# Router logits of two steps summed in PSUM and selected by two products: a retention and two-level expert kernel

## The chip, the cores and the metric

The kernel runs on one core of one Trainium2 chip. The metric is the device time of the whole program in microseconds (us), as the median of several runs. A profiled execution is traced by the hardware profiler; its span, and the time of every instruction in it, count from its first to its last record. TensorE is PE in the rows (PEld for its weight loads, which run beside its products), VectorE is DVE, ScalarE is ACT, GpSimd is POOL, and SyncE, whose queue issues nearly all DMA, is SP.

## The reference

A retention attention (4 batches, 8 heads, 768 tokens, heads of 64 wide) makes x, 3072 tokens of 512 columns. Each token then chooses one of 4 groups and in it one of 4 experts, and is sent through that one expert alone.

```python
for t in range(S):                                    # per batch and head
    state = gamma * state + k[t] v[t]^T
    y[t] = scale * q[t] state
x = y, tokens of all batches x (H*D)                  # 3072 x 512
g_logits = x @ w_group                                # 4 logits
e_logits = x @ w_expert[g]                            # 4 logits for each of 4 groups
g, e = argmax of g_logits, argmax of e_logits of group g
out = softmax(g_logits)[g] * softmax(e_logits)[e] * (relu(x @ w1[g, e]) @ w2[g, e])
```

So each token has 20 router logits: 4 of the groups and 16 of the experts. They are what the change is about.

## The kernel before, in words

**The steps.** The attention runs in 12 steps i = 0 to 11. A step has 256 tokens, as two blocks u = 0 and 1 of 128 tokens; six steps (NC) make up one pass over the 768 tokens for half of the batches. In a step TensorE does, in the order in which the loop of `attention` writes it:

- `scores(i + 1, 0)` and `scores(i + 1, 1)`: the score products of the next step (L240) into the four PSUM banks `sh[0]` to `sh[3]`, two for each block. VectorE then masks each bank into `pf` (L252). In the rows the four banks are sh, in the order sh_116 to sh_119.
- `state_out(i, u)` (L291) and `value_out(i, u)` (L304): the output of the step, summed in PSUM as op, on four 64 x 64 quadrants and on halves of TensorE.
- `state_mm` (L266): keys times values into the state stp, which ScalarE copies to V (L276). The keys kk are transposed on TensorE and copied by ScalarE (`keys_mm`, L225, L226), but for steps 9 and 10 (KEYED), whose keys are loaded a second time, by DMA (L217), into the one buffer that kk has.
- `logits_mm(i - 1)` (L324): the router logits of the step before, see below, and their copy `ls` by ScalarE (L329).
- `out_x(i)`: VectorE scales op to `xt` (L316), the step's x, 512 columns in four groups of 128 rows by its 256 tokens. xt has two buffers.
- `trans_mm(i - 1)`: xt is transposed into the banks sh[2] and sh[3] (L350), ScalarE copies it to `xr` (L358), and a DMA writes it to memory as `xd` (L361), from which the tokens of an expert are gathered later. For step 10 that copy goes to a buffer of pf.

**The logits before.** The router weights `wr` are 128 x 4 x 32 (20 of the 32 columns in use). For each of the four groups j of x's columns one product of 32 stationary columns and 256 moving ones (the tokens) goes to its own 32 rows of PSUM:

```python
nc.tensor.matmul(
    lt[32 * j:32 * j + 32, :], self.wr[:, j, :], s["xt"][:, j].rearrange("p u t -> p (u t)"),
    start=True, stop=True, skip_group_check=True,
)
```

So the four partial sums of a logit stand in four row groups. `select_mm` (L337) adds them up and turns the result to tokens by logits: for each block the 128 x 128 piece of ls is the stationary operand and a constant of 128 x 20, which is 1 where row s has s % 32 equal to the column (`C_SEL`), the moving one. It writes 20 columns of the bank `log`. In most steps it stands inside `trans_mm`; in four steps it is held back as `late` and done in the next step by `select_late`. The product of the last step goes to a bank lgt of its own, with the tag "sta".

**Routing.** A batch is four blocks, two steps. `route` is a list of stages that `route_steps` lets run on from places in the loop: the maxima and marks on VectorE (from the logits in `log`, with the exponential ex on ScalarE, L396, and the marks oh, L408), the ranks on TensorE (L444, L446), the offsets on VectorE (L452 to L461), the weights. `spread` makes the lists' marks (hot on VectorE, ent on GpSimd, yT on VectorE) and `tally` (L555) counts them up on TensorE into the lists from which the tokens are gathered.

**Expert weights beside it.** Through all of this the expert weights come in as wf by DMA and are split in two parts: wh by ScalarE (L784), wl by VectorE (L786). The first expert layer (L918) starts after step 11; the first gather (L821) and its transposes (L839) stand ahead of it.

**What sets the order.** The schedule is manual: each engine does its instructions in the order in which the program writes them. SP's queue, too, issues the loads and the writes of xd in that order. A tile with one buffer is written again only when its last reader is done; the program waits on semaphores for that.

Of the kernel before, what the change touches and what calls it, by code (L numbers as in the profile page):

```python
# [51 lines left out]
C_DESC = C_TB + NL  # L52
C_SEL, C_SEG = C_DESC + 20, C_DESC + 40
C_KP, C_WP, C_IT = C_SEG + NX, C_SEG + 2 * NX, C_SEG + 3 * NX
# [17 lines left out]
def constants():  # L72
    s = np.arange(P)
    g = 1.0 - 2.0 ** (-5.0 - np.arange(H))
    c = np.zeros((P, C_REST + C_END), np.float64)
    n = np.arange(NC)[None, :, None] * P + KEYS.T[:, None, :] + 1.0
    c[:, C_GV:C_GV + NC * H] = (g ** -n).reshape(P, NC * H)
    for half in range(2):
        c[64 * half:64 * half + 64, C_GS:C_GS + 4] = g[[h[half] for h in HEAD]] ** P
    d = c[:, C_REST:]  # L80
    d[:, C_IO:C_IO + P] = s[None, :]
    d[:, C_PI] = s
    d[:, C_CH:C_CH + NCH] = P * (np.arange(NCH) - 32)
    d[:, C_TB:C_TB + NL] = (np.arange(NX)[:, None] * CAP + np.arange(2) * P).reshape(-1)
    d[:, C_DESC:C_DESC + 20] = [4, 3, 2, 1] * 5
    d[:, C_SEL:C_SEL + 20] = s[:, None] % 32 == np.arange(20)[None, :]
    d[:, C_SEG:C_SEG + NX] = np.arange(NX) * CAP
    d[:, C_KP:C_KP + NX] = np.arange(NX)
    d[:, C_WP:C_WP + NX] = PW
    d[:, C_IT:C_IT + MAXI] = np.arange(MAXI)  # L90
    return c.astype(np.float32)
# [20 lines left out]
class Kernel:  # L112
    def __init__(self, tc, qkv, kt, wr, w1p, w2p, cst, dec, out):
# [6 lines left out]
        self.held = None  # L120
        self.late = None
        self.waiting = False
# [186 lines left out]
    def out_x(self, i):  # L309

        s = self.st[i]
        s["xt"] = xt = self.wp.tile([P, 4, 2, P], F32, name="xt", bufs=2)
        for par in range(2):
# [3 lines left out]

    def logits_mm(self, i, bank=None):

        nc, s = self.nc, self.st[i]  # L320
        lt = self.pp.tile([P, 512], F32, name="lgt", tag="sta", bufs=1) if bank is None else self.sh[bank]
        lt = lt[:, 0:2 * P]
        for j in range(4):
            nc.tensor.matmul(  # L324
                lt[32 * j:32 * j + 32, :], self.wr[:, j, :], s["xt"][:, j].rearrange("p u t -> p (u t)"),
                start=True, stop=True, skip_group_check=True,
            )
        s["ls"] = self.wp.tile([P, 2 * P], F32, name="ls", bufs=1)
        nc.scalar.activation(s["ls"], lt, AF.Copy)  # L329

    def select_mm(self, i):

        nc, s = self.nc, self.st[i]
        for u in range(2):
            a = LG + 20 * (i % 2 * 2 + u)
            lg = self.log[:, a:a + 20]
            nc.tensor.matmul(lg, s["ls"][:, u * P:u * P + P], self.rest[:, C_SEL:C_SEL + 20], start=True, stop=True)  # L337

    def select_late(self):
        if self.late is not None:  # L340
            self.select_mm(self.late)
            del self.st[self.late]
            self.late = None

    def trans_mm(self, i, pool=None, late=False):

        nc, s = self.nc, self.st[i]
        for u in range(2):
            for j in range(4):
                nc.tensor.transpose(self.sh[2 + u][:, j * P:j * P + P], s["xt"][:, j, u], self.ident)  # L350
        if not late:
            self.select_mm(i)
        if i == NS2 - 2:
# [814 lines left out]
    def attention(self, extra, beside):  # L1168
# [27 lines left out]
        for i in range(NS2):  # L1196
# [10 lines left out]
            if i:  # L1207
                if i > 2:
                    self.outs(i)
                if i > 1:  # L1210
                    scores(i + 1, 0)
                if i % 2 and not last:
                    self.select_late()
                if i in (5, 7, 9):
                    self.tally()
                if i > 2:
                    self.state_out(i, 0)
                if last:
                    self.select_late()
                if i > 1:  # L1220
                    self.state_out(i, 1)
                if i < NS2 - 2:
                    self.select_late()
                if i % 2 == 0:
                    self.route_steps(99, True)
                if i > 1:
                    scores(i + 1, 1)
            self.load("q", i + 3)
            self.load("v", i + 3)
# [9 lines left out]
            self.state_copy(i)  # L1239
            if i == 10:  # L1240
                self.select_late()
            beside(i, 4)
            if i:
                self.logits_mm(i - 1, 1 if last or i % NC == NC - 2 or i + 1 in KEYED else 2)
            self.out_x(i)
# [26 lines left out]
            if i:  # L1272
                late = i + 1 in KEYED or i % NC == NC - 2
                self.trans_mm(i - 1, late=late)
                if late:
                    self.late = i - 1
                else:
                    del self.st[i - 1]
            if last:
# [27 lines left out]
    def run(self):  # L1307
        tc, nc = self.tc, self.nc
        with ExitStack() as ctx:
# [87 lines left out]
            hot = self.marks(p)  # L1397
            self.logits_mm(last)
            self.xtrans(ua, "big", (0,))
            self.select_mm(last)  # L1400
            self.trans_mm(last, self.yp, late=True)
            self.wload(va, 2)
# [161 lines left out]
```

## Time and profile before

| | us |
|---|---|
| median of 3 runs | 394.56 (394.51 to 395.0) |
| the profiled execution | 392.61 |
| its span | 390.9 |
| TensorE, products | 381.9 busy, 98% of the span |
| TensorE, weight loads | 322.9, 83% |
| VectorE | 288.5, 74% |
| ScalarE | 224.3, 57% |
| GpSimd | 160.2, 41% |

The mean granted clock of TensorE is 0.994 of full speed. The attention with the routing of the first five batches takes the span up to about 103 us; the rest are expert layers.

How to read the views. The view by windows gives a stretch, its width, the busy time of PE, PEld, DVE, ACT and POOL with the instructions of each, the granted clock of TensorE (1.00 is full), the share of time in which the 16 DMA engines were busy, and GB/s. The DMA view gives output and input, queue, the number of issues, the size of each and the median time from issue to landing. The chain of waits goes back from the last instruction to what released it, at each step; the timeline lists groups of alike instructions by their start, with their length. A bracket behind a row is the idle time of the engine ahead of it and what ended it.

### The profile page before, as it was taken

To read this page: it belongs to the slowest core of one execution; us is meant where nothing else is said; L and a number is where in the kernel's file an instruction comes from. 1 tells how busy PE (TensorE), PEld (TensorE's weight loads), DVE (VectorE), ACT (ScalarE), POOL (GpSimd) and SP (SyncE) were. 2 spreads that over 40 slices of the span, in tenths; PEclk is the share of its full clock that TensorE was granted. 3 is DMA by queue.
4 is the path that set the end of the run, shared out by engine and by line. 5 is a ranking of instruction groups with operands and counts; after the bars stand their busy time and mean duration, and the time that the engine had idled before them with its cause. 6 is when DMAs were issued, how large, how long until landed. Compare 5 with 4: busy or idle time off the path is not lost.

```text
span 390.9 us, 14282 instructions
## 1 busy us (share of the span) xinstructions
PE 381.9 (98%) x5945; PEld 322.9 (83%) x5977; DVE 288.5 (74%) x480; ACT 224.3 (57%) x342; POOL 160.2 (41%) x172
## 2 busy tenths in 40 slices
PE   8999999999999999999999999999999999999993
PEld 4888989888869888888888879797887978879792
DVE  3675876868879979795868686776878769788630
ACT  2234534544654766666657667676766767667620
POOL 5533669578766325131425324241531403322112
PEclk9999999999999999999999999999999999999997
DMA  7999999989647998787879797988879798797011
GB/s 254 342 369 325 315 381 321 341 292 305 221 177 259 338 359 269 249 278 257 268 249 274 268 331 251 300 294 305 293 262 352 273 314 300 268 349 263 6 49 50
DMA packets 38042, 107.24 MB, mean 274 GB/s; under 512 B 11415, under 2 KB 11543, under 8 KB 30548
## 3 DMA queue, kind: packets, MB, share of 16 engines
q1 hardware_dynamic: 28752, 92.52, 68.5%
q0 software_dynamic: 8928, 12.63, 9.2%
q8 instruction: 54, 0.88, 0.9%
q10 hardware_dynamic: 292, 1.08, 0.8%
q14 instruction: 16, 0.13, 0.1%
HBM read 94.18 MB, written 13.20 MB: 275 GB/s over the span
## 4 chain that ended last, share of the span: by engine, by line
PE 83%; issue 9%; POOL 3%; DMA 3%; DVE 0%; POOLq 0%; ACT 0%; SPq 0%; DVEq 0%; ACTq 0%
PE hps L918 19%; PE yps L1011 16%; PE hps L898 9%; PE yps L1016 6%; PE op L304 5%; PE sh L240 4%; PE yps L1004 3%; PE tpx L839 3%; PE sh L350 3%; PE stp L266 3%; PE op L291 2%; POOL out L1098 2%; DMA kk<-kt 2%; PE sh L324 1%; PE yps L955 1%
## 5 line engine op out<-in xcount | busy, mean ns | idle before, releaser
L786 DVE TENSOR_TENSOR wl<-wf,wh 128x1024 bf16<-128x1024 f32 x120 | 145.3, 1222 | 38.5 <-ACT wh L784 38.2
L784 ACT ACTIVATE wh<-wf 128x1024 f16<-128x1024 f32 (+1 forms) x136 | 133.6, 1002 | 1.0 <-DMA wf<-w2p 1.0
L918 PE MATMUL hps<-xbh,wh 128*128 128x0 bf16 x544 | 93.3, 241 | 0.0
L918 PE MATMUL hps<-xbh,wl 128*128 128x0 bf16 x544 | 93.3, 241 | 0.0
L1098 POOL DMA_INDIRECT out<-yo,mt x18 | 22.2, 1235 | 102.9 <-ACT yo L1078 100.1
L918 PEld LDWEIGHTS <-wh 128*128 128x128 f16 x616 | 56.5, 98 | 0.1
L925 ACT ACTIVATE hh<-hps 128x256 bf16<-128x256 f32 (+16 forms) x68 | 34.2, 503 | 35.6 <-PE hps L918 35.3
L918 PEld LDWEIGHTS <-wl 128*128 128x128 bf16 x544 | 53.2, 98 | 0.2
L898 PE MATMUL hps<-xbl,wh 128*128 128x256 f16 (+14 forms) x472 | 50.2, 249 | 0.0
L1016 PEld LDWEIGHTS <-wh 128*128 128x128 f16 x448 | 28.6, 97 | 24.9
L252 DVE TENSOR_TENSOR pf<-sh,tri 128x512 f32<-128x512 f32 x48 | 30.6, 685 | 21.8 <-PE sh L240 7.8
L1011 PE MATMUL yps<-wh,hl 128*128 128x512 f16 x112 | 42.5, 380 | 0.0
L1011 PE MATMUL yps<-wl,hh 128*128 128x512 bf16 x112 | 42.4, 379 | 0.0
L1011 PE MATMUL yps<-wh,hh 128*128 128x512 f16 x112 | 42.4, 378 | 0.0
L821 POOL DMA_INDIRECT xg<-xd,mt x22 | 36.8, 1674 | 11.0 <-PE hps L898 2.7
L841 ACT ACTIVATE xbh<-tpx 128x512 bf16<-128x512 f32 (+14 forms) x32 | 16.7, 523 | 42.7 <-PE tpx L839 42.6
L898 PEld LDWEIGHTS <-wh 128*128 128x128 f16 x472 | 40.2, 98 | 0.5
L1016 PEld LDWEIGHTS <-wl 128*128 128x128 bf16 x448 | 28.6, 97 | 13.3
L928 DVE SCALAR_TENSOR_TENSOR hl<-hps,hh 128x216 f16<-128x216 f32 (+15 forms) x64 | 36.8, 576 | 2.7 <-ACT hh L925 2.6
L1098 POOL DMA_INDIRECT out<-yo,gx x8 | 9.5, 1194 | 55.6 <-ACT yo L1078 41.4
L1016 PE MATMUL yps<-hh,wh 128*128 128x0 bf16 x448 | 31.8, 192 | 0.0
L1016 PE MATMUL yps<-hh,wl 128*128 128x0 bf16 x448 | 31.7, 192 | 0.0
(210 smaller groups left out, 632.6 us busy)
## 6 DMA issues: line engine op xcount, KB each, us to landing
wf<-w2p SPq DMA_DIRECT2D x29, 1024.0 KB, 6.3
wf<-w1p SPq DMA_DIRECT2D x28, 1024.0 KB, 6.9
lq<-qkv SPq DMA_DIRECT2D x24, 256.0 KB, 5.8
lk<-qkv SPq DMA_DIRECT2D x24, 256.0 KB, 5.3
lv<-qkv SPq DMA_DIRECT2D x24, 256.0 KB, 5.8
xd<-xr SPq DMA_DIRECT2D x22, 256.0 KB, 4.9
wf<-w1p SPq DMA_DIRECT2D x16, 256.0 KB, 5.9
wf<-w2p SPq DMA_DIRECT2D x8, 256.0 KB, 5.9
```

The source lines that it names most:

```text
L252: nc.vector.tensor_tensor(o, sc, tri, ALU.mult)
L304: nc.tensor.matmul(s["o"][par][64 * half:64 * half + 64, u, pp], s["vs"][:, u, hs], s["pf", u][:, par, p, :], start=(c == 0 and u == 0 and ...
L784: nc.scalar.activation(u["wh"][i][:, cs], u["wf"][i][:, cs], AF.Copy)
L786: (eng or nc.vector).tensor_tensor(u["wl"][i][:, cs], u["wf"][i][:, cs], u["wh"][i][:, cs], ALU.subtract)
L821: nc.gpsimd.indirect_dma_start(out=xg[0:r, i, :], out_offset=None, in_=self.xd[0:n, :], in_offset=bass.IndirectOffsetOnAxis(ap=mt[0:r, i, ...
L898: nc.tensor.matmul(hv[:, a, 0:w], l, xl[:, k, 0:w], start=(k == 0 and a == 0), stop=False, skip_group_check=True)
L918: nc.tensor.matmul(o, l[:, k, fs], m, start=(n == 0 and not arms), stop=(n == len(terms) - 1), skip_group_check=True,)
L925: nc.scalar.activation(hh[:, f, 0:W], hv[:, :, 0:W], AF.Relu)
L928: nc.vector.scalar_tensor_tensor(*rest)
L1011: nc.tensor.matmul(big, h[:, k, 0:P], w[k], start=(n == 0), stop=(n == 23))
L1016: nc.tensor.matmul(o, w[k][:, d * P:d * P + P], m, start=(n == 0 and d == 0), stop=(n == 23), skip_group_check=True,)
L1098: s = nc.gpsimd.indirect_dma_start(out=self.out, out_offset=bass.IndirectOffsetOnAxis(ap=mt[0:r, i, 0:1].bitcast(U32), axis=0), in_=yo[0:r ...
```

## The change

Three things are changed.

- **The products.** `pair_logits(i - 2)` takes the place of `logits_mm`. It runs in even steps i only, behind `scores(i + 1, 1)` and ahead of `value_out`, and does the logits of two steps, i - 2 and i - 1. Each of the four blocks of 128 tokens (two steps, two blocks) has its own 32 rows of PSUM, and the four column groups of x are summed there, in four products of 128 moving columns: 16 products in all. The result is 128 x 128, in bank sh[0]; that of the last pair, after the loop, is in lgt. ScalarE's copy ls is 128 x 128.
- **The selection.** `pair_select` takes the place of `select_mm` and `select_late`. It runs behind `state_copy` of even steps. With 64 columns of ls, twice, as the stationary operand and 80 columns of the unit matrix as the moving one, it turns the logits of 64 tokens of four blocks at once. `trans_mm` has no selection any more.
- **The constants.** `C_SEL` goes, 20 columns of 128 x 4 bytes, 10 KB.

```diff
-    def logits_mm(self, i, bank=None):
-        nc, s = self.nc, self.st[i]
-        lt = self.pp.tile([P, 512], F32, name="lgt", tag="sta", bufs=1) if bank is None else self.sh[bank]
-        lt = lt[:, 0:2 * P]
-        for j in range(4):
-            nc.tensor.matmul(
-                lt[32 * j:32 * j + 32, :], self.wr[:, j, :], s["xt"][:, j].rearrange("p u t -> p (u t)"),
-                start=True, stop=True, skip_group_check=True,
-            )
-        s["ls"] = self.wp.tile([P, 2 * P], F32, name="ls", bufs=1)
-        nc.scalar.activation(s["ls"], lt, AF.Copy)
-    def select_mm(self, i):
-        nc, s = self.nc, self.st[i]
-        for u in range(2):
-            a = LG + 20 * (i % 2 * 2 + u)
-            lg = self.log[:, a:a + 20]
-            nc.tensor.matmul(lg, s["ls"][:, u * P:u * P + P], self.rest[:, C_SEL:C_SEL + 20], start=True, stop=True)
+    def pair_logits(self, i):
+        nc = self.nc
+        if i == NS2 - 2:
+            lt = self.pp.tile([P, 512], F32, name="lgt", tag="sta", bufs=1)[:, 0:P]
+        else:
+            lt = self.sh[0][:, 0:P]
+        for g in range(4):
+            for j in range(4):
+                nc.tensor.matmul(
+                    lt[32 * j:32 * j + 32, :], self.wr[:, g, :], self.xts[i + j // 2][:, g, j % 2],
+                    start=(g == 0), stop=(g == 3), skip_group_check=True,
+                )
+        self.ls = self.wp.tile([P, P], F32, name="ls", bufs=1)
+        nc.scalar.activation(self.ls, lt, AF.Copy)
+    def pair_select(self):
+        pick = self.ident.rearrange("p (j c) -> p j c", j=4)[:, :, 0:20]
+        for a in (0, 64):
+            lg = self.log[a:a + 64, LG:LG + 80].rearrange("p (j c) -> p j c", j=4)
+            self.nc.tensor.matmul(lg, self.ls[:, a:a + 64], pick, start=True, stop=True, skip_group_check=True)
...
-        if not late:
-            self.select_mm(i)
...
                 if i > 1:
                     scores(i + 1, 1)
+                if i % 2 == 0:
+                    self.pair_logits(i - 2)
...
             self.state_copy(i)
-            if i == 10:
-                self.select_late()
+            if i and i % 2 == 0:
+                self.pair_select()
             beside(i, 4)
-            if i:
-                self.logits_mm(i - 1, 1 if last or i % NC == NC - 2 or i + 1 in KEYED else 2)
             self.out_x(i)
...
-            self.logits_mm(last)
+            self.pair_logits(last - 1)
             self.xtrans(ua, "big", (0,))
-            self.select_mm(last)
-            self.trans_mm(last, self.yp, late=True)
+            self.pair_select()
+            self.trans_mm(last, self.yp)
```

TensorE's order at two places. First step 10, from the last score product of step 11 (lq and lk are its queries and keys, sh_119 is bank sh[3]) to the tally. Before:

```order
L240 MATMUL sh_119<-lq,lk 64x64
L304 MATMUL op<-pf,vs 64x128 x16
L266 MATMUL stp<-vs,kk 64x64 x16
L337 MATMUL log<-rest,ls 128x20 x2
L324 MATMUL sh_117<-xt,wr 32x256 x4
L555 LDWEIGHTS hot
```

And of the changed kernel, where sh_116 is bank sh[0]:

```order
L239 MATMUL sh_119<-lq,lk 64x64
L326 MATMUL sh_116<-xt,wr 32x128 x16
L303 MATMUL op<-pf,vs 64x128 x16
L265 MATMUL stp<-vs,kk 64x64 x16
L338 MATMUL log<-ident,ls 64x80 x2
L548 LDWEIGHTS hot
```

The logits product has moved from behind the state product to ahead of value_out, as one of 16 instructions, into the bank in which the first scores of step 11 stand until VectorE's mask has read them.

Then the end of step 11 and what stands ahead of the first expert layer (lgt is the last product's bank, tpx the transposes of the gathered tokens xg, wh the expert weights). Before:

```order
L350 MATMUL sh_118<-ident,xt 128x128 x4
L350 MATMUL sh_119<-ident,xt 128x128 x4
L337 MATMUL log<-rest,ls 128x20 x2
L324 MATMUL lgt<-xt,wr 32x256 x4
L839 MATMUL tpx<-ident,xg_80 128x128 x4
L337 MATMUL log<-rest,ls 128x20 x2
L350 MATMUL sh_118<-ident,xt 128x128 x4
L350 MATMUL sh_119<-ident,xt 128x128 x4
L918 LDWEIGHTS wh
```

And of the changed kernel:

```order
L345 MATMUL sh_118<-ident,xt 128x128 x4
L345 MATMUL sh_119<-ident,xt 128x128 x4
L326 MATMUL lgt<-xt,wr 32x128 x16
L832 MATMUL tpx<-ident,xg_80 128x128 x4
L338 MATMUL log<-ident,ls 64x80 x2
L345 MATMUL sh_118<-ident,xt 128x128 x4
L345 MATMUL sh_119<-ident,xt 128x128 x4
L911 LDWEIGHTS wh
```

The selection behind the transposes of step 10 is gone, and the last product, now of steps 10 and 11, has 16 instructions in place of 4. On VectorE the mask that reads bank sh[0] in step 10 stands, before as now, behind the offsets of the ranks (L452 to L461), the weights of the batch and the marks for the lists (yT and hot). On VectorE, ScalarE, GpSimd and SP the order is as before, but that the copies ls are six in place of twelve and move with their products.

## Rows read from the trace of the kernel before

**Rows 1.** The page, section 1: busy time, share of the span, instructions

```profile
PE 381.9 (98%) x5945; PEld 322.9 (83%) x5977; DVE 288.5 (74%) x480; ACT 224.3 (57%) x342; POOL 160.2 (41%) x172
```

**Rows 2.** The view by windows, 6 to 84 us (columns: section on profile)

```profile
6.00:84.00 78.00, 77.36 (x1770) 68.24 (x1764) 52.99 (x125) 31.84 (x64) 47.78 (x62) 1.00 1.00 343
```

**Rows 3.** The DMA view, 6 to 84 us: count, size, median us to landing

```profile
lv<-qkv SPq DMA_DIRECT2D x22, 256.0 KB, 5.8
...
kk<-kt SPq DMA_DIRECT2D x2, 256.0 KB, 6.3
```

**Rows 4.** The DMA view, 100 to 104 us

```profile
xd<-pf SPq DMA_DIRECT2D x2, 256.0 KB, 2.1
```

**Rows 5.** The chain of waits, steps 7 to 10: start us, us, what

```profile
71.27 0.36 PE log L337 x4
...
76.03 0.93 PE stp L266 x32
...
77.59 6.23 DMA kk<-kt
...
83.87 1.33 PE stp L266 x32
...
92.25 0.55 PE log L337 x4
```

**Rows 6.** The waits of the weight loads, 0 to 105 us: us, times, longest

```profile
PEld stp L266 <- DMA kk<-kt: 0.3, 1, 0.3
```

**Rows 7.** The timeline, steps 2 to 4: start us, us, engine, line, instruction

```profile
29.31 0.16 PEld L324 LDWEIGHTS sh<-xt,wr 128*32 128x32 f32 x8
...
29.32 0.64 PE L324 MATMUL sh<-xt,wr 128*32 128x256 f32 x8
...
29.88 0.85 PEld L225 LDWEIGHTS sh<-ident,lk 128*128 128x128 f32 x8 [0.41 <-issue]
...
40.92 0.90 PEld L291 LDWEIGHTS op<-lq,V 64*64 64x64 f32 x32
```

**Rows 8.** The timeline, end of step 9 to the first expert layer

```profile
83.06 1.29 DVE L252 TENSOR_TENSOR pf<-sh,tri 128x512 f32<-128x512 f32 x2 [2.10 <-PE op L304]
...
86.63 0.20 PE L444 MATMUL log<-oh,stri 128*128 128x80 bf16 x1
...
87.52 0.22 DVE L452 TENSOR_TENSOR log<-log,nb 128x64 f32<-128x64 f32 x1
...
89.35 1.73 PEld L304 LDWEIGHTS op<-pf,vs 128*64 128x64 f32 x32
...
91.05 2.47 DVE L252 TENSOR_TENSOR pf<-sh,tri 128x512 f32<-128x512 f32 x4
...
94.28 1.08 ACT L358 ACTIVATE xr<-sh 128x512 f32<-128x512 f32 x2 [0.45 <-PE sh L350]
...
95.25 1.15 ACT L784 ACTIVATE wh<-wf 128x512 f16<-128x512 f32 x2
...
96.63 0.24 ACT L396 ACTIVATE ex<-log 128x80 f32<-128x80 f32 x1 [0.23 <-PE op L291]
...
97.94 0.23 DVE L408 TENSOR_TENSOR oh<-log,go 128x64 bf16<-128x64 f32 x1
...
98.97 0.10 PEld L444 LDWEIGHTS <-stri 128*128 128x128 bf16 x1 [0.41 <-issue]
...
99.31 0.23 DVE L452 TENSOR_TENSOR log<-log,nb 128x64 f32<-128x64 f32 x1
...
101.75 0.52 PEld L337 LDWEIGHTS log<-rest,ls 128*128 128x128 f32 x4 [0.21 <-ACT ls L329]
...
103.02 0.10 PEld L918 LDWEIGHTS <-wh 128*128 128x128 f16 x1
```

**Rows 9.** The view by windows, near the end of the span

```profile
387.00:388.00 1.00, 0.00 (x0) 0.00 (x0) 0.00 (x0) 0.00 (x0) 0.00 (x0) 0.50 0.28 111
```

**Rows 10.** The instructions of line 324 (xt product): shortest, median, longest ns

```profile
L324 PEld LDWEIGHTS sh<-xt,wr x88: 106/108/110, 19.4 to 98.4; 128*32 128x32 f32 x88
```

More of the change, by code (lines that the diff above doesn't have):

```diff
@@ L52 @@
 C_DESC = C_TB + NL
-C_SEL, C_SEG = C_DESC + 20, C_DESC + 40
+C_SEG = C_DESC + 20
 C_KP, C_WP, C_IT = C_SEG + NX, C_SEG + 2 * NX, C_SEG + 3 * NX
@@ L85, in constants @@
     d[:, C_DESC:C_DESC + 20] = [4, 3, 2, 1] * 5
-    d[:, C_SEL:C_SEL + 20] = s[:, None] % 32 == np.arange(20)[None, :]
     d[:, C_SEG:C_SEG + NX] = np.arange(NX) * CAP
@@ L120, in __init__ @@
         self.held = None
-        self.late = None
+        self.xts = {}
         self.waiting = False
@@ L311, in out_x @@
         s = self.st[i]
-        s["xt"] = xt = self.wp.tile([P, 4, 2, P], F32, name="xt", bufs=2)
+        s["xt"] = self.xts[i] = xt = self.wp.tile([P, 4, 2, P], F32, name="xt", bufs=2)
         for par in range(2):
@@ L316, in out_x, with trans_mm @@
             self.nc.vector.tensor_tensor(xt[:, gs], s["o"][par].rearrange("p u g t -> p g u t"), g, ALU.mult)
-    def logits_mm(self, i, bank=None):
-        nc, s = self.nc, self.st[i]
-        lt = self.pp.tile([P, 512], F32, name="lgt", tag="sta", bufs=1) if bank is None else self.sh[bank]
-        lt = lt[:, 0:2 * P]
-        for j in range(4):
-            nc.tensor.matmul(
-                lt[32 * j:32 * j + 32, :], self.wr[:, j, :], s["xt"][:, j].rearrange("p u t -> p (u t)"),
-                start=True, stop=True, skip_group_check=True,
-            )
-        s["ls"] = self.wp.tile([P, 2 * P], F32, name="ls", bufs=1)
-        nc.scalar.activation(s["ls"], lt, AF.Copy)
-    def select_mm(self, i):
-        nc, s = self.nc, self.st[i]
-        for u in range(2):
-            a = LG + 20 * (i % 2 * 2 + u)
-            lg = self.log[:, a:a + 20]
-            nc.tensor.matmul(lg, s["ls"][:, u * P:u * P + P], self.rest[:, C_SEL:C_SEL + 20], start=True, stop=True)
[L339 to L345, printed above, removed]
+    def pair_logits(self, i):
[17 more added lines that the diff above has]
+            self.nc.tensor.matmul(lg, self.ls[:, a:a + 64], pick, start=True, stop=True, skip_group_check=True)
+    def trans_mm(self, i, pool=None):
         nc, s = self.nc, self.st[i]
@@ L1211, in attention @@
                     scores(i + 1, 0)
-                if i % 2 and not last:
-                    self.select_late()
                 if i in (5, 7, 9):
@@ L1217, in attention @@
                     self.state_out(i, 0)
-                if last:
-                    self.select_late()
                 if i > 1:
                     self.state_out(i, 1)
-                if i < NS2 - 2:
-                    self.select_late()
                 if i % 2 == 0:
@@ L1239, in attention @@
             self.state_copy(i)
-            if i == 10:
-                self.select_late()
+            if i and i % 2 == 0:
+                self.pair_select()
             beside(i, 4)
-            if i:
-                self.logits_mm(i - 1, 1 if last or i % NC == NC - 2 or i + 1 in KEYED else 2)
             self.out_x(i)
@@ L1272, in attention @@
             if i:
[L1273 to L1278, printed above, removed]
+                self.trans_mm(i - 1)
+                del self.st[i - 1]
             if last:
```

## The prediction

> **What bounds the kernel now.** I read the page first. The reader is to see that TensorE counts as busy for 98% of the span [rows 1], which would make every TensorE instruction taken away a gain. So I next asked what paces the stretch that the change touches, steps 0 to 11 (to about 103 us). The view by windows answers: from 6 to 84 us the 16 DMA engines are busy for a share of 1.00 at 343 GB/s [rows 2]. They are not only busy but backed up: in that stretch a 256 KB load lands 5.8 us after its issue (median of 22), the keys of step 9 (kk) 6.3 us after it [rows 3], while a 256 KB write issued when the engines are idle lands after 2.1 us [rows 4]. The chain of waits shows where the backlog meets TensorE: one step of it is no TensorE work but the load of kk for step 9, 77.59 to 83.82, behind which state_mm(9) starts at 83.87 [rows 5]. TensorE waited only 0.3 us for it [rows 6], so two paths arrive together: TensorE's own and the DMA's. All loads and writes stand in SP's queue in one order that the change leaves alone, and so do their bytes (the constants shrink by 10 KB, under 0.03 us). Engines that are busy all the time don't finish the same bytes sooner because they are asked sooner. I take kk of step 9 to land at 83.8 as before.
>
> **What the change takes from TensorE.** A logits product of one step holds TensorE from 29.31 to the next load at 29.88 [rows 7]: 0.57 us, 12 times, 6.8 us. A selection costs 0.36 us on the chain where it stands behind the transposes, 0.55 us where it stands late [rows 5]; four of the twelve are late ones, so about 5 us. New are six logits products of a pair: 16 matmuls of 128 columns on four column groups. The nearest row is state_out, 16 matmuls of 128 columns on four 64 x 64 quadrants, whose loads span 0.90 us [rows 7]. The other end is the old product scaled by its columns: twice 0.57, 1.14 us. I take 1.0, the nearer to state_out since its columns agree. The new selection is two products of 64 stationary and 80 moving columns: at most the old 0.36 us; at least 0.12 us, four of the 32 passes that state_mm does in 0.93 us (76.03 in [rows 5]; two passes make one fp32 product). I take 0.27, nearer to the old one, since two products in a row hide little. Six pairs: 7.6 us against 11.8 us before, so TensorE loses 4.2 us of work. ScalarE's copy of the logits becomes one of 128 columns for two of 256; it is on no path that I found.
>
> The four column groups do overlap in the trace: all eight weight loads of an old product are issued within 0.16 us of 29.31, and eight passes take 0.64 us in all [rows 7]. [...]
>
> **Up to 83.87: nothing.** By state_mm(9) TensorE is rid of eight logits products (4.6 us) and six or seven selections (some 2.7 us) and has four pairs more (5.1 us): 2.2 us ahead, less what it loses to short waits for VectorE on the way, some 2 us. All of it ends in the wait for kk of step 9. Gain 0, at most the 0.3 us by which it waited already.
>
> **From 83.87 on, step by step against the old trace** [rows 8].
> - Step 9 ends without its logits product: the ranks (L444) stand at 86.05 in place of 86.63. VectorE is ready for them: its mask for step 10 waited for value_out(9), which is now about 2 us earlier, so the marks (oh) and xt(9) are done before the ranks.
> - A new wait. In step 10 the pair product of steps 8 and 9 is written into bank sh[0], and the scores of step 11 are still in that bank until VectorE's mask has read them. Its order there is unchanged: after the ranks come offsets, weights, the list marks and then the mask. Before, from L452 at 87.52 to the end of the first of four masks was 91.05 + 0.62 - 87.52 = 4.15 us. L452 can now start about 0.35 us after the ranks (98.97 to 99.31 shows that step), at 86.4, so the bank is free at 90.55. TensorE is there 2.72 us after the ranks (86.63 to 89.35), at 88.77, and waits 1.8 us. Queued behind it: value_out(10), state_mm(10), the selection, the tally, the transposes of xt(9). A gain is excluded, since the order on VectorE stands; I keep 1.3 us (half a microsecond less for marks that GpSimd slows) to 2.9 us (VectorE not ahead, the bank free at 91.67 as before).
> - So value_out(10) starts at 90.55 + 1.0 = 91.55, 2.2 us later than 89.35.
> - From there to ScalarE's copies xr(9) it was 4.93 us (to 94.28); a late selection and a logits product go (1.12 us), the new selection comes (0.27): 4.1 us, xr(9) at 95.6, 1.35 late.
> - ScalarE does in order xr(9), the weights wh, then the exponential ex. Before, ex did not wait for wh (95.25 + 1.15 = 96.40) but for VectorE, at 96.63. Now wh ends at 97.75 and ex starts at 97.8: 1.2 us late. The marks (oh) end 1.54 us behind the start of ex, at 99.35, in place of 98.17.
> - The last ranks waited for nothing at 98.97, since a logits product stood ahead of them; now they wait for oh until 99.4: 0.45 late.
> - From these ranks to the first expert layer (L918) it was 4.05 us. Out go a selection (0.55), a logits product (0.57), a selection (0.36) and a wait of 0.2 for ScalarE; in come a pair (1.0) and a selection (0.27): 3.65 us. L918 starts at 103.05 in place of 103.02.
> - The route of the last batch hangs on VectorE's split of the gathered tokens, which follows the gather's transposes, 0.35 us late; its ranks had about 0.2 us to spare inside L918, so 0.1 to 0.2 us more.
>
> The sum is +0.2 us: gain and new wait cancel. Behind 103 us TensorE has no wait in the trace and its instructions are the same, so the shift stays. The profiled execution took 392.61 us (span 390.9 and 1.7 around it), 1.95 us below the median of 394.56 of the runs shown; I carry the shift to the median: **394.7 us**. With each term at its ends (pair 0.9 to 1.14 twice, wait at sh[0] 1.3 to 2.2, selection 0.12 to 0.36 twice) the case reaches from 394.0 to 395.6.
>
> **Rivals.**
> - *The load is not fixed.* If kk of step 9 lands as much earlier as its issue moves (about 2 us), the whole end moves by that: 394.7 - 2 = 392.8. For it: it is issued when state_mm(8) is done, and that comes earlier. Against: share 1.00 and a latency nearly three times that of an idle moment.
> - *TensorE is the bound throughout and the bank is free in time:* all 4.2 us are gained, 390.4. Against: the same rows, and the mask's place on VectorE.
> - *Slower: the wait at sh[0] in full.* If xt(9) isn't done when the ranks of step 9 come, VectorE's queue stands as before, the bank is free at 91.67 in place of 90.55, and all behind it is 1.1 us later: 395.9. It decides at value_out(9, 0): VectorE needs 4.5 us from there until it is free for L452 (83.06 to 87.52), so it must end by 81.9 (before: 83.0). TensorE being 2 us ahead speaks for 81, but the tally of step 9 and the copies xr(7), which wait for GpSimd and for DMA writes, can eat that lead.
> [...]
> - *The groups don't overlap when they add up in PSUM* (no row shows 32-column groups that accumulate over four products). One after another, at 0.106 us a pass (eight passes of 128 columns, loads from 29.88 within 0.85 us), a pair costs 3.4 us in place of 1.0: two behind 83.87 give +4.8 us, 399.5. If only a load of 0.108 us stands ahead of each of the eight sets [rows 10], a pair is 0.86 us longer and the sum 1.7 us: 396.4.
>
> [...]
>
> **How the numbers follow.** Forecast 0.65; load not fixed 0.13; all gained 0.03; sh[0] in full 0.10; clock 0.05; groups or loads in series 0.04. A measurement of this kernel tells 0.2% from no change, 0.8 us: same is 393.8 to 395.35. Faster: 0.13 + 0.03 + 0.03 of the forecast's low end = 0.19. Slower: 0.10 + 0.05 + 0.04 and 0.04 of its high end = 0.23. Same: 0.58. The range 392.8 to 396.0 takes in the forecast's own (394.0 to 395.6), the load that isn't fixed and sh[0] in full, 0.88 together; the rest stays out.
>
> **What would show it.** Right: state_mm(9) still starts near 83.8, with about 2 us of waiting for kk ahead of it; the pair product in step 10 waits 1.3 to 2.2 us for a mask (L251 in the new numbering) and then takes about 1.0 us; ex of the fifth batch starts right behind wh; the first expert layer starts within 0.6 us of 103.0; all behind it has the old length. Wrong: state_mm(9) at 82 or earlier (the load moved), a pair product of 1.5 us or more (groups in series), a clock below 1.00 before 300 us, or a first expert layer before 102.2.

## The result, and the profile after

| kernel | median us | range, executions | ratio to before, 95% interval |
|---|---|---|---|
| before | 394.63 | 394.34 to 395.2, 6 | |
| changed | 399.58 | 397.39 to 401.95, 6 | 1.0129 (1.0096 to 1.0163) |

The changed kernel is slower by 1.3%, 5 us. The forecast was 394.7 with a range up to 396.0, so it was wrong. A ratio here and below leaves out executions that lie over 1.5% above the fastest one of their kernel; a median does not. Single executions of the changed kernel lie 4.6 us apart, those of the kernel before 0.9 here, though up to 8.3 (392.99 to 401.28, 29 executions) in a later comparison. The traced execution is the longest of the six, 401.95 us (span 400.2), and that of before the shortest shown, 392.61: the difference of the traces, 9.3 us, is more than that of the medians, and sizes below are read with that in mind.

The head of the page after, for [rows 1]:

```profile
span 400.2 us, 14370 instructions
...
PE 378.0 (94%) x5974; PEld 323.4 (81%) x6049; DVE 287.1 (72%) x480; ACT 221.2 (55%) x336; POOL 160.9 (40%) x172
...
q8 instruction: 55, 0.90, 0.9%
```

TensorE has less to do, 378.0 us for 381.9, and is idle for 22 us of the span in place of 9. The first expert layer, for the last row of [rows 8], starts at 110.96 in place of 103.02:

```profile
110.96 0.10 PEld L911 LDWEIGHTS <-wh 128*128 128x128 f16 x1
```

So 7.9 of the 9.3 us are lost in the attention. Of the 1.4 behind it 0.5 are one wait of a tally for GpSimd (to 122.1), and 0.7 stand behind TensorE's last product. What TensorE waited for up to there, from the view of waits (engine, what it was to write, line, what ended the wait: us in all, times, the longest):

```profile
PE sh L326 <- issue: 3.3, 1, 3.3
PE sh L326 <- DVE pf L251: 3.1, 2, 2.3
PE op L303 <- issue: 1.3, 1, 1.3
PE log L437 <- DVE oh L401: 1.3, 2, 0.7
...
PE log L548 <- POOL yT L527: 0.8, 1, 0.8
PE op L290 <- issue: 0.6, 1, 0.6
```

In the trace of before, from 6 to 104 us, the same view has two rows:

```profile
PE op L291 <- issue: 0.4, 1, 0.4
PE sh L350 <- ACT ls L329: 0.2, 1, 0.2
```

There are two kinds. The waits for pf, oh and yT are waits for another engine: 5.2 us. The other kind, "issue", is one in which TensorE waits for nothing that the profile shows: 5.3 us. The longest stands in the middle of a pair product, in step 8. The timeline (start, us, engine, line, instruction, and the idle time ahead of it):

```profile
75.26 0.36 PEld L326 LDWEIGHTS sh<-xt,wr 128*32 128x32 f32 x11
75.27 0.62 PE L326 MATMUL sh<-xt,wr 128*32 128x128 f32 x10
...
79.24 0.85 PE L326 MATMUL sh<-xt,wr 128*32 128x128 f32 x22 [3.35 <-issue]
79.24 0.58 PEld L326 LDWEIGHTS sh<-xt,wr 128*32 128x32 f32 x21 [3.62 <-issue]
...
80.02 3.26 PE L303 MATMUL op<-pf,vs 128*64 128x128 f32 x32
```

Ten of the 32 passes run, then TensorE stands still for 3.35 us, and goes on. Both steps' xt have been read by the first eight passes already, and the view names no other engine whose work ends the wait. The value_out behind it takes 3.26 us, where those of the next three steps take 1.97; the view by windows (columns as in [rows 2]) shows why:

```profile
80.00:81.00 1.00, 1.00 (x17) 0.98 (x16) 0.00 (x0) 0.28 (x1) 0.00 (x0) 0.75 1.01 352
81.00:82.00 1.00, 1.00 (x13) 1.00 (x10) 0.31 (x1) 0.00 (x0) 0.00 (x0) 0.50 0.53 197
82.00:83.00 1.00, 1.00 (x13) 1.00 (x12) 1.00 (x3) 0.00 (x0) 0.00 (x0) 0.50 0.06 25
83.00:84.00 1.00, 1.00 (x24) 1.00 (x22) 1.00 (x2) 0.00 (x0) 0.00 (x0) 0.54 0.02 6
84.00:85.00 1.00, 1.00 (x27) 0.91 (x24) 0.97 (x3) 0.40 (x1) 0.49 (x1) 1.00 0.00 0
```

From 80.5 on, 1.3 us behind the end of the standstill, the granted clock is at 0.50 for 3.4 us, and back at 1.00 from 83.9. It costs 1.6 us: on the chain of waits value_out takes 3.19 in place of 1.90 and state_mm 1.27 in place of 0.93.

### The profile page after: what moved, and what is told of

It reads as the page before. It is cut to its first block, busy times and chain, and to the rows that moved or that the text cites. A ratio compares the mean times of both kernels' runs of the same rounds, so it can differ in the third digit from the quotient of the medians.

```text
span 400.2 us, 14370 instructions
## 1 busy us (share of the span) xinstructions
PE 378.0 (94%) x5974; PEld 323.4 (81%) x6049; DVE 287.1 (72%) x480; ACT 221.2 (55%) x336; POOL 160.9 (40%) x172
## 3 DMA queue, kind: packets, MB, share of 16 engines
q10 hardware_dynamic: 292, 1.08, 0.9%
## 4 chain that ended last, share of the span: by engine, by line
PE 74%; issue 12%; DVE 7%; POOL 4%; DMA 1%; ACT 1%; POOLq 0%; SPq 0%; DVEq 0%
PE hps L911 18%; PE yps L1004 14%; PE hps L891 9%; PE yps L1009 7%; PE op L303 5%; PE sh L239 4%; PE yps L997 3%; PE tpx L832 3%; PE op L290 2%; POOL out L1091 2%; PE stp L265 2%; DVE pf L251 2%; PE sh L326 1%; PE sh L345 1%; PE sh L224 1%
## 5 line engine op out<-in xcount | busy, mean ns | idle before, releaser
L814 POOL DMA_INDIRECT xg<-xd,mt x22 | 37.7, 1715 | 15.3 <-PE yps L1035 4.7
L196 POOL TENSOR_TENSOR vs<-lv,cst 128x512 f32<-128x512 f32 x24 | 24.6, 1040 | 15.2 <-DMA lv<-qkv 11.7
```

The costliest lines, as they stand in the source:

```text
L196: self.nc.gpsimd.tensor_tensor(o, v, g, ALU.mult)
L814: nc.gpsimd.indirect_dma_start(out=xg[0:r, i, :], out_offset=None, in_=self.xd[0:n, :], in_offset=bass.IndirectOffsetOnAxis(ap=mt[0:r, i, ...
```

## The experiments

Two theories. **M (masks):** in its new place and bank, and with TensorE freed of work, the pair product makes TensorE wait for VectorE's masks and marks; "issue" is incidental. **F (instruction fetch):** TensorE's program comes in by DMA while it runs, in the blocks that the page lists as "q8 instruction", 55 of 16 KB here (that they are TensorE's is inferred), behind the same loads that keep the DMA engines busy (a share of 0.95 from 6 to 84 us here); where TensorE gets through a block before the next one is there, it stands still. The expectations call these standstills stalls. The pair products bring more instructions, and so they bring more of this.

All runs in one table; ratios are to the kernel before on the same chip. "Fetch" is the sum of TensorE's standstills by issue of over 0.1 us from 6 us to the first expert layer (neither a product nor a weight load under way), "others" that of its waits for other engines and loads, each from the one trace of the run. The traced execution is the longest or second longest of its run in changed, after_again, both splits, ahead and light_ahead, and one of the shorter ones in the rest. So the sums are those of one execution and not of the median; how much a kernel loses is read from the times.

| run | median us | ratio, 95% interval | fetch us | others us |
|---|---|---|---|---|
| before | 394.63 | | 0.4 | 0.2 |
| before_again (one execution) | 393.45 | | 1.2 | 0.2 |
| changed | 399.58 | 1.0129 (1.0096 to 1.0163) | 5.3 | 5.2 |
| after_again | 400.92 | 1.0126 (1.0087 to 1.0164) | 5.8 | 4.9 |
| split_before | 398.94 | 1.0091 (1.0058 to 1.0125) | 5.7 | 1.3 |
| split4_before | 401.26 | 1.0138 (1.0074 to 1.0202) | 7.5 | 0.2 |
| eight | 399.18 | 1.0117 (1.0071 to 1.0163) | 3.0 | 5.3 |
| ahead | 397.89 | 1.0070 (1.0036 to 1.0104) | 8.0 | 1.1 |
| eight_ahead | 394.83 | 1.0004 (0.9974 to 1.0035) | 0.6 | 2.3 |
| light_ahead | 395.56 | 1.0012 (0.9978 to 1.0045) | 4.2 | 3.2 |
| light_before | 394.51 | 0.9989 (0.9962 to 1.0016) | 1.9 | 0.1 |
| ranks_later | 396.92 | 1.0031 (1.0005 to 1.0057) | 1.2 | 1.3 |

**The changed kernel again.**

> The changed kernel as it is, for a second trace. [...] F expects 1 to 5 us of such stalls ahead of 103 us again, at other places than 75.89, a clock below 1.00 behind one of over 3 us, and single times spread over some 4 us. Theory M (masks): the time goes into waits for VectorE, of the pair products for the masks in sh[0] and of the ranks for oh; M expects the same waits as before, 0.7 us in step 6 and 2.3 us in step 10, and issue stalls under 0.5 us in all. Both: 397.4 to 402, median 399.6.

Measured: 400.92 (395.9 to 408.28). The traced execution is its longest, so its places are read and not its sizes. The waits for masks stand where they stood, 0.74 us in step 6 and 2.34 in step 10; the standstills by issue have moved, to 39.6 (0.5 us), 45.6 (1.7), 52.1 (1.1) and, in the pair product of step 8 again, 81.4 (2.3). The granted clock falls to 0.50 twice here, from 84.2 on, behind that standstill, and from 104.7 on, behind the wait for the mask in step 10, which ends at 103.30:

```profile
105.00:106.00 1.00, 1.00 (x14) 1.00 (x12) 0.00 (x0) 0.00 (x0) 1.00 (x2) 0.50 0.97 375
106.00:107.00 1.00, 1.00 (x12) 1.00 (x10) 0.93 (x2) 0.00 (x0) 0.66 (x1) 0.50 0.98 377
```

M's part repeats, F's comes and goes with the execution, and so does the time. Both are there; the next runs part them.

**More instructions, nothing else.** The kernel before, with each logits product split by token block:

```diff
-                lt[32 * j:32 * j + 32, :], self.wr[:, j, :], s["xt"][:, j].rearrange("p u t -> p (u t)"),
+                lt[32 * j:32 * j + 32, 0:P], self.wr[:, j, :], s["xt"][:, j, 0],
...
+        for j in range(4):
+            nc.tensor.matmul(
+                lt[32 * j:32 * j + 32, P:2 * P], self.wr[:, j, :], s["xt"][:, j, 1],
...
```

> The kernel before with each logits product of 256 columns split into two of 128 columns, so that TensorE streams the same columns with 16 more instructions of weight loads and products (as the trace counts them) in a step; nothing waits for anything new. F: more instructions per microsecond, so stalls by issue and a wider spread: 396 to 399 us. M: within 0.2% of the kernel before, 394.2 to 395.4, since TensorE's work and the waits stand (the loads add at most 0.1 us a step, 1.2 us in all, if they are not hidden).

Measured: 1.0091, some 3.6 us slower, with no pair and no new place. The products themselves are 0.5 us of it (7.3 us by start to start in its trace, 6.8 before). From the view of waits, 6 to 104 us:

```profile
PE op L291 <- issue: 2.6, 2, 2.2
PE op L304 <- issue: 2.3, 2, 1.3
PE stp L266 <- DMA kk<-kt: 1.1, 1, 1.1
PE stp L266 <- issue: 0.5, 1, 0.5
...
```

The wait of 1.1 us is for the keys of step 9, on which TensorE's loads waited 0.3 us before. The first long standstill on the timeline, and the DMA view of the 0.2 us in which the block's transfer starts (packets, MB, share of 16 engines):

```profile
28.07 0.34 PE L291 MATMUL op<-lq,V 64*64 64x128 f32 x4 [2.21 <-issue]
...
q8 instruction: 1, 0.02, 32.7%
```

TensorE stands still from 25.86 to 28.07. The block's packet starts between 25.5 and 25.7; a share of 32.7% of 16 engines over 0.2 us is 1.05 us, so it has landed at about 26.6, and TensorE goes on 1.4 us later. In the changed kernel the same: packet at 76.8, TensorE on again at 79.24:

```profile
q8 instruction: 1, 0.02, 30.5%
```

That is 30.5% of 16 engines over 0.2 us, 0.98 us: landed at 77.8, 1.5 us before TensorE goes on. And no other such packet started from 67.6 until then. In the twelve traces 45 standstills of over 0.2 us between 6 us and the first expert layer are put down to issue, and each ends 1.2 to 1.6 us behind the landing of a block; the waits for other engines and loads end anywhere from 0.2 to 6.9 us behind one. For 35 of the 45 an earlier block is in the trace. From 1.4 us behind that one's landing until the standstill ends the traces have never fewer than 248 products and loads of TensorE (median 256), where a block holds some 220 on average: no standstill comes before about a block has been used up. So F's mechanism is shown, as far as TensorE waits for its blocks; that they are late because of the loads is tried below.

**Three times the added instructions.** As above, with four products of 64 columns each.

```diff
-        for j in range(4):
-            nc.tensor.matmul(
-                lt[32 * j:32 * j + 32, :], self.wr[:, j, :], s["xt"][:, j].rearrange("p u t -> p (u t)"),
+        for u in range(2):
+            for h in range(2):
+                for j in range(4):
+                    a = u * P + 64 * h
+                    nc.tensor.matmul(
+                        lt[32 * j:32 * j + 32, a:a + 64], self.wr[:, j, :], s["xt"][:, j, u, 64 * h:64 * h + 64],
```

> The kernel before with each logits product of 256 columns split into four of 64, three times the instructions that the split into two added (576 in place of 192). F: the loss grows with the instructions, by about 0.019 us for each: +9 to +12 us over the kernel before, 403 to 407, with fetch stalls of 12 us or more. If the loss of the split into two had another cause (the added weight loads themselves, 0.02 us each where TensorE issues them), it would be the products that take longer, not the stalls: stalls as in the split into two, and the products of a step 0.5 us longer.

Measured: 1.0138, 5.4 us (2.9 to 8.0 by the interval), not the 9 to 12 that F was to give. The standstills do grow, from 5.7 to 7.5 us in the traces, but far from threefold. The products are not what grew: 7.6 us by start to start, for 7.3 with the split into two. F names the mechanism; a price for each instruction does not follow from it. That what TensorE loses at one block gives the next one time to come would fit this; it was not tried.

**Half the instructions of the pair, in its place.**

```diff
-        for g in range(4):
...
-                    lt[32 * j:32 * j + 32, :], self.wr[:, g, :], self.xts[i + j // 2][:, g, j % 2],
-                    start=(g == 0), stop=(g == 3), skip_group_check=True,
+        for k in range(2):
...
+                g = 2 * (j // 2) + k
...
+                    lt[32 * j:32 * j + 32, :], self.wr[:, g, :], self.xts[i + j % 2][:, g].rearrange("p u t -> p (u t)"),
+                    start=(k == 0), stop=(k == 1), skip_group_check=True,
...
+        pick = self.wr[:, :, 20:30].rearrange("p (s e) r -> p s e r", s=2)
+        for u in range(2):
+            lg = self.log[:, LG:LG + 80].rearrange("p (s v e r) -> p s v e r", s=2, v=2, e=2)[:, :, u]
+            self.nc.tensor.matmul(lg, self.ls[:, u * P:u * P + P], pick, start=True, stop=True)
```

The selection's constant, pick, has ones at two row groups of 32 for each logit; it is made once, in columns of wr that were zero.

> The changed kernel with the product of a pair done as 8 products of 256 columns in place of 16 of 128: each of the four column groups holds one step and two of the four groups of x, and the selection adds two row groups up. Place, bank and streaming time of the pair product stay (1.03 us), its instructions are halved. F: the stalls go back, 396 to 398, with less spread. M: the time of the changed kernel, 399 to 400, and the waits for masks at the pair products of steps 6 and 10 as before.

Measured: 399.18, M's time and not F's, with 3.0 us of standstills in its trace for 5.3:

```profile
PE sh L333 <- DVE pf L257: 3.1, 2, 2.3
PE sh L245 <- issue: 1.7, 1, 1.7
PE log L444 <- DVE oh L408: 1.3, 2, 0.7
PE op L296 <- issue: 1.2, 1, 1.2
PE log L555 <- POOL yT L534: 1.0, 2, 0.5
```

With the waits for masks in place it stays slow, though some standstills are left as well.

**The pair ahead of state_out, in another bank.**

```diff
                 if i in (5, 7, 9):
                     self.tally()
+                if i % 2 == 0:
+                    self.pair_logits(i - 2)
                 if i > 2:
                     self.state_out(i, 0)
...
-                if i % 2 == 0:
-                    self.pair_logits(i - 2)
...
-            lt = self.sh[0][:, 0:P]
+            lt = self.sh[2][:, 0:P]
```

> The changed kernel with the pair product moved ahead of state_out and into bank sh[2], which is free there, so that value_out no longer stands behind a mask of the next step; the second score product now waits for ScalarE's copy ls in its place. M: the waits for masks go (0.7 and 2.3 us) and with them most of the loss: 395 to 397. F: the instructions are as many and as dense, so 398 to 400, with stalls by issue.

Measured: 397.89, between the two. The wait for pf is gone, that for ls in its place is 0.4 us, and standstills by issue are nearly all that is left, on six different lines:

```profile
PE sh L239 <- issue: 3.8, 3, 1.6
PE op L290 <- issue: 2.0, 3, 0.9
PE sh L326 <- issue: 0.8, 1, 0.8
PE log L437 <- DVE oh L401: 0.7, 1, 0.7
PE stp L265 <- issue: 0.6, 1, 0.6
PE log L338 <- issue: 0.5, 1, 0.5
PE sh L224 <- issue: 0.4, 1, 0.4
PE sh L239 <- ACT ls L331: 0.4, 1, 0.4
```

With 8.0 us they are more than in the changed kernel, in an execution that is 3 us above the median.

**Both.** The diffs of eight and ahead together, the product in sh[2] with 256 columns.

> Both edits together: 8 products of 256 columns for a pair, ahead of state_out, in bank sh[2]. [...] Theory M (waits for masks alone): the time of the run with the product ahead, 397 to 399, since its waits are the same.

Measured: 394.83, 1.0004 (0.9974 to 1.0035): the loss is gone. F is right here, and M's 397 to 399 wrong: with the waits for masks gone, 192 instructions taken away are worth 3 us (397.89 to 394.83), near the 3.6 us that 192 more cost in split_before, where with those waits in place they were worth nothing that could be told (eight). The waits that are left:

```profile
PE log L444 <- DVE oh L408: 1.6, 3, 0.7
PE op L296 <- issue: 0.6, 1, 0.6
PE log L555 <- POOL yT L534: 0.6, 2, 0.3
PE sh L245 <- ACT ls L338: 0.5, 1, 0.5
```

So there are two causes, the place and bank (M) and the number of instructions (F). With the waits for masks kept and the pair's instructions halved the loss is 1.2% (eight), with those waits gone and the instructions kept 0.7% (ahead), with both there 1.3%, less than the sum; only with both taken away it is gone. That each hides part of the other, since a wait for VectorE gives a block time to land, fits these four times; no run shows it by itself. Nor does a run part the number of instructions from the places at which the blocks end among them; that one program's standstills move from execution to execution (after_again) speaks for the number.

**Less DMA, the same instructions.** The loads of the first expert's weights in steps 2 to 9 are left out of the run with the pair ahead of state_out, and out of the kernel before as a control; their buffers are zeroed once.

```diff
     def wload_part(self, u, k):
         i, h = divmod(k, 4)
+        if u["e"] == 0:
+            return
...
             if i == 1:
                 self.const_pieces()
+                beside(i, 6)
...
+                if place == 6:
+                    ua["wh"], ua["wl"] = [None] * 4, [None] * 4
+                    ua["wf"] = [self.wst.tile([P, 2048], F32, name="wf", tag="wf", bufs=4) for _ in range(4)]
+                    for k in range(4):
+                        (nc.vector if k % 2 else nc.gpsimd).memset(ua["wf"][k], 0.0)
```

> The run with the pair product ahead of state_out (16 products, bank sh[2]), with less DMA: the 16 loads of 256 KB of the first expert's weights in steps 2 to 9 are left out, and the four buffers are zeroed once in step 1 instead; TensorE's instructions are the same. Theory F (a block of instructions lands late because its fetch stands behind the loads): with some 4 of 27 MB gone the backlog shrinks; the stalls ahead of the first expert layer fall from 8.0 us to 0 to 3, and the time from 397.9 to 392 to 395. If the blocks came late for another reason (a fixed rate of fetching, whatever the loads), the stalls stay at 6 to 8 us and the time within 1 us of 397.9.

> The control: the kernel before with the same 16 loads left out. Its trace has under 1.5 us of fetch stalls, so F leaves it little to gain: 393.5 to 394.6. The prediction's own bound (the keys of step 9 that land late) gives at most the 0.3 us that state_mm waited. A gain of over 2 us would say that the loads hold the kernel before back by another path as well.

Measured: 395.56 where the same instructions with all loads took 397.89, and 394.51 for the control, which gains nothing. The window of 6 to 84 us (columns as in [rows 2]) with all loads (ahead) and then without the 16:

```profile
6.00:84.00 78.00, 72.71 (x1713) 64.40 (x1705) 50.42 (x121) 29.64 (x60) 43.27 (x57) 1.00 0.98 329
6.00:84.00 78.00, 71.92 (x1680) 64.60 (x1673) 52.46 (x121) 27.77 (x56) 45.36 (x58) 0.98 0.84 278
```

The DMA share is 0.84 in place of 0.98, and the standstills fall from 8.0 to 4.2 us, not to the 0 to 3 expected; the time misses F's 392 to 395 by half a microsecond. Of the 4.2 us 1.7 stand at 14.7 us, ahead of the first load that is left out (26.4 in ahead); behind it 2.5 are left of 7.1. Time and standstills fall where TensorE's instructions are the same, as F has it and a fixed rate of fetching has not. That the other two are left (28.5 and 77.7) fits the DMA engines still being busy for 0.9 of the stretch from 20 to 30 us and 0.88 from 70 to 80; that is read from one trace and was not tried. Two things weaken it. The control's trace has 1.9 us of standstills, more than the 0.4 and 1.2 of the two traces with all loads. And the zeroing is work that the other run has not, four instructions of 1.8 us on VectorE and GpSimd between 21.6 and 31.5. So the loads' part rests above all on the time of light_ahead, in one comparison.

**A try at more.** Both edits, and the ranks moved from the end of an odd step to behind the first score product of the next.

```diff
-            if i == 10:
-                self.route_steps(99, True)
-                self.spread(3)
...
                     scores(i + 1, 0)
+                if i > 2 and i % 2 == 0:
+                    self.route_steps(99, True)
+                if i == 10:
+                    self.route_steps(99, True)
+                    self.spread(3)
...
-            if i % 2 and not last:
-                self.route_steps(99, True)
```

> Eight products, ahead of state_out, and the ranks of a batch moved from the end of an odd step to behind the first score product of the next (in step 10 the marks of the lists move with them). In the run without this move TensorE waited 0.7 and 0.6 us at the ranks for oh, 0.5 us for ls and twice 0.3 us at the tally. F: instructions unchanged and few enough, so the 1.3 us at the ranks are gained: 393.3 to 394, ahead of the kernel before by 0.1 to 0.4%. If the wait is only handed on (VectorE's masks come behind the ranks' offsets, later), 394.5 to 395.5.

Measured: 396.92, 1.0031 (1.0005 to 1.0057), rather slower. The wait for oh falls from 1.6 to 0.3 us and nothing is gained. Of the two expectations that of a wait handed on is nearer, though the time is above it too.

**The kernel before again.**

> The kernel before for a second trace. F: its instructions come just in time, so this trace may show stalls of 1 to 3 us that end 1.3 to 1.6 us behind the landing of a block, where its time is above 394; M has none. The first expert layer between 103 and 106.

393.45 us, its first expert layer at 104.25, with two standstills, 0.9 and 0.3 us. The kernel before meets the fetch too, now and then.

None of the variants beats the kernel before.

## Why the prediction was wrong, point by point

- **Cost of the new products: right.** A pair product takes 1.01 to 1.08 us on the chain (1.0 forecast), and the four column groups do overlap when they add up in PSUM. The 32 loads of a pair, of 128 rows each, fit into 0.81 us beside its products (the row at 98.42 below), so no load stands ahead of each of the eight sets of four passes. The rivals with groups or loads in series (3.4 and 1.9 us) are out. A selection costs 0.14 on the chain (0.27 forecast, from 0.12 to 0.36).
- **The work taken away: right, and it did not matter.** By start to start of TensorE's records ahead of the first expert layer, standstills left out, logits products and selections took 12.3 us before and 8.3 after, 4.0 less; 4.2 was the forecast.
- **"Up to 83.87: nothing", the step that failed.** It had TensorE 2 us ahead at step 9, waiting for kk. State_mm(9) starts at 90.26 where 83.87 was forecast, and kk is in no wait:

```profile
90.26 1.07 PEld L265 LDWEIGHTS stp<-vs,kk 128*64 128x64 f32 x32
```

  TensorE has lost more than it gained by then: the standstills by issue (0.6, 1.3 and 3.35 us), the clock behind the last (1.6), and waits of 0.8 for yT, 0.7 for oh and 0.7 for pf in steps 5 and 6. These are 9.1 us; less the 2.2 of saved work and the 0.6 of waits of the old trace, 6.3 are left of a delay of 6.4. From there to value_out(10) another 1.5 us are lost (99.44, forecast 91.55), and from there to the first expert layer nothing (11.5 us, as forecast). So the failed step carries most of the loss. The sum had no term for instructions at all, though it counted them: 8 products for 2 steps became 16, and the view of [rows 7] shows each as weight loads and passes. "Short waits for VectorE on the way" were allowed for inside the 2 us and took more than that.
- **kk as a bound: not tested by the change.** In the changed kernel TensorE comes to state_mm(9) later than kk. It does not land at a fixed time either: issued between 77.60 and 89.11 in seven traces, it lands 2.8 to 7.3 us later, so it moves when its issue moves late; no run shows it moving early. That light_before gains nothing (0.9989) decides nothing, since the forecast gave at most the 0.3 us of [rows 6] for it.
- **The wait at sh[0] in step 10: right in place, and its size partly by luck.** It took 2.34 us, where 1.8 was the value, 1.3 to 2.2 the sum's range and 2.9 the rival's end:

```profile
92.98 1.28 DVE L315 TENSOR_TENSOR xt<-op,gx 128x512 f32<-128x512 f32 x2
94.18 0.22 DVE L445 TENSOR_TENSOR log<-log,nb 128x64 f32<-128x64 f32 x1
...
97.69 1.28 DVE L251 TENSOR_TENSOR pf<-sh,tri 128x512 f32<-128x512 f32 x2
...
98.42 0.81 PEld L326 LDWEIGHTS sh<-xt,wr 128*32 128x32 f32 x32 [2.50 <-DVE pf L251]
...
99.44 1.73 PEld L303 LDWEIGHTS op<-pf,vs 128*64 128x64 f32 x32 [0.20 <-issue]
```

  The product begins when the first of the masks is through, and value_out behind it. But VectorE was not ahead, as the forecast had it: the ranks of step 9 waited 0.6 us for oh (to 93.12), and xt(9) stood between them and the offsets (L445), which began 1.1 us behind the ranks in place of 0.35. That is the condition of the rival "sh[0] in full". From the start of the offsets to the end of the first mask it took 4.2 us, for 4.15 in the forecast. The half microsecond for which the forecast has GpSimd slow the marks is in both traces: in step 10 yT takes 0.79 us on VectorE (L527 before, L520 now) while GpSimd splits wl, and 0.26 to 0.28 the other four times. Its smaller twin in step 6 (0.74 us) was not foreseen.
- **ScalarE's chain behind it: right in kind.** The ex of the fifth batch starts at 105.39, within 0.2 us of the end of the two wh that begin at 104.35 and take 1.15.
- **The 0.05 for the clock: it did fall.** Of the rows of before only [rows 9] have it below 1.00, where TensorE has no work left; that it falls behind TensorE's waits was the author's estimate. In the first trace it fell in step 8, behind a standstill of 3.35 us, and stayed at 1.00 behind the 2.34 us in step 10; in after_again it fell behind that very wait too. In the twelve traces it falls to 0.50 five times ahead of the first expert layer, each time behind a wait, of 1.7 to 3.35 us (two in after_again, one each in changed, split4_before and light_ahead); behind others, 2.21 us in split_before and 2.34 in eight, it does not.
- **The range** had only causes that the trace of before could show as waits. A term for instruction blocks, some 3 us by ahead against eight_ahead, would have given a rival that is slower. One slip is without weight: the low ends of its terms lead to 393.8, not 394.0.

What stays open is where the 3.7 us of saved work go in eight_ahead, whose first expert layer starts at 103.88. 2.4 us more are waits (0.6 and 2.3 us, for 0.4 and 0.2). By start to start, the score products take 1.4 and the transposes 1.0 us more than before: the records of `scores(i + 1, 0)` take 0.63 us where state_out follows them at once, and 0.83 where the pair product does. That is the account of one trace, and no run tried it.

## To carry to other kernels

In these runs the blocks of TensorE's program came in among the loads, and standstills behind them took up to 8.0 us ahead of the first expert layer, at a DMA share of 0.98 (ahead). So count the instructions that an edit adds beside their time: eight products of 256 columns in place of 16 of 128 were worth 3 us there (397.89 to 394.83). When the profile says that TensorE waited for "issue" for a microsecond or more, look at the packets of the instruction queue before looking at the code: all 45 such standstills of over 0.2 us here ended 1.2 to 1.6 us behind the landing of one. And a product that is moved ahead of other work can meet the last reader of the bank that it is written into, as in step 10, where that took 2.34 us: ask when that bank is free before choosing the place. (The run ahead changed place and bank together; no run parts them.)

## What the runs showed of the hardware

- TensorE's program arrives during the run: 54 packets of 16 KB on q8 before, 55 after, about one for 220 of its products and loads (0.88 MB by 54 is 16.4 KB each; that they are TensorE's is inferred from its standstills). A packet takes about 1 us to move (0.98 and 1.05 above), and where TensorE stands still for one, it goes on 1.2 to 1.6 us behind its landing. The standstills cost up to 8.0 us in 100 at a DMA share of 0.98 (ahead), and 0.4 us in the trace of before at a share of 1.00.
- With the same loads and the same columns streamed, 192 instructions more cost 3.6 us (2.3 to 4.9, split_before), and 576 cost 5.4 (2.9 to 8.0, split4_before): not a price per instruction.
- One standstill of 3.35 us cost about 5, with the clock's 1.6 behind it.
